# Chunked attention inside a fused transformer block: one exponential per tile, with VectorE subtracting the maximum and summing, in place of eight per-head exponentials

## The chip, the cores and the metric

One Trainium2 chip; the program runs on one core. The metric is device time in microseconds (us) of one execution. The engines are TensorE (PE for its matmuls, PEld for its weight loads), VectorE (DVE), ScalarE (ACT), GpSimd (POOL) and SyncE (SP), which issues the loads and stores.

## The reference

Shortened here. Attention runs within chunks of 64 tokens, for 8 heads of 64 columns, on 8 batches of 576 tokens. Two feed-forward parts follow, a plain one and one gated by a causal convolution.

```python
scores = scale * np.matmul(q_c, k_c.transpose(0, 1, 2, 4, 3))
scores = scores - np.max(scores, axis=-1, keepdims=True)
attn = np.exp(scores)
attn = attn / (np.sum(attn, axis=-1, keepdims=True) + 1e-09)
out = np.matmul(attn, v_c)
...
xn = (x - mu) / np.sqrt(var + 1e-06) * g_ln
ch = np.maximum(xn @ w_ch1, 0.0) @ w_ch2      # x is (8, 576, 512), w_ch1 (512, 2048)
x = x + ch
...
gate = 1.0 / (1.0 + np.exp(-gate_pre))        # gate_pre: causal convolution of x, 5 taps
out = gate * (x @ w_val) @ w_out
```

## The kernel before

The 4608 tokens are cut into 36 tiles of 128 rows (two chunks each); a tile's attention and normalization is called a unit, `unit(u)`. Four units feed one block of 512 tokens, and there are 9 blocks, 0 to 8. Blocks 0 and 1 go through the feed-forward part as plain products (`ffn`), blocks 2 to 8 as seven products of halved matrices (`operands`, `hidden`). After each block comes the convolution and the preparation of the gated part (`conv`, `seven`), and after the last block the gated part itself (`val`, `proj`). Matmul operands are split into a high and a low part, so that each product is three matmuls.

The order of all work is made ahead, by a planner (`Plan`). Every operation is added with an engine, an estimated duration, the operations that it waits for, and a priority; `run` replays this as a greedy schedule, and the instructions are written in the order that comes out. On the chip each engine works through its list in that order and waits on semaphores, so the estimates set the order, and the chip's own durations set the time. The units of a block are planned well ahead of the block, between the products of the blocks before, with priorities that put them ahead of the convolution.

Units 0 to 7 (`u < MERGED`) use an older path. There `smax` (L579) takes the maximum and subtracts it in two DVE instructions, `sexp` (L591) makes one exponential, and the sum of P comes out of a matmul with a column of ones. Units 8 to 35, 28 in all, use the path that the change touches:

- `burst` (L542): one stretch of PE work that writes P times V of the unit before (`pv_plain`) and the scores of this unit into the two banks of one PSUM tile, `att` (64x64 matmuls, L531).
- `peak` (L556, DVE): the maximum of each head's 64 scores (L558), times -1/8 (L559).
- `weigh` (L561, ACT): for each of 8 heads an exponential of 128x64 out of PSUM (L567), with the maximum as bias and the sum of P as accumulator output; the profile shows each as an ACTIVATE and an ACTIVATION_READ_ACCUMULATOR.
- `ev_x` (L606, DVE), for the unit before: reciprocal of the sums, x = (P times V) times it (L616), then the statistics of the normalization (L624 to L627).
- `rstd` (L629, POOL) and `norm` (L633, DVE): xn.
- `tr_p` (L594, PE) turns P by four 128x128 transposes (L504) into the PSUM tile, `ev_p` (L597, ACT) copies it out over P (L598).
- `tr_n` (L639, PE) turns x and xn of the unit before into the same PSUM tile (L504); ACT copies them out (L654, L682).

The tile library adds the waits. It puts PSUM reads of ACT and DVE in the order in which the instructions were written, when they read the same PSUM tile: where x (L616) is written ahead of the first exponential, the exponential waits for it.

Of the kernel before, what the change touches and what calls it, by code (L numbers as in the profile page):

```python
# [9 lines left out]
F32 = mybir.dt.float32  # L10
# [3 lines left out]
AF = mybir.ActivationFunctionType  # L14
ALU = mybir.AluOpType
AX = mybir.AxisListType

P = 128
CH = 64
# [12 lines left out]
class Plan:  # L32
# [8 lines left out]
    def add(self, eng, dur, fn, deps=(), pri=0.0):  # L41
        op = Op(eng if isinstance(eng, tuple) else (eng,), dur, fn, deps, pri, len(self.ops))
        self.ops.append(op)
        return op

    def take(self, tag):

        return self.held.get(tag, [])

    def hold(self, tag, *ops):  # L50
        self.held[tag] = list(ops)
# [55 lines left out]
def chunk_attention_ffn_gated_conv(  # L107
# [21 lines left out]
    nc = tc.nc  # L129
    B, H, S, D = q.shape  # L130
# [9 lines left out]
    HP = H // 2  # L140
    SCALE = 1.0 / float(D) ** 0.5
# [36 lines left out]
    def view(t, shape, dt):  # L178
        n = 1
        for x in shape[1:]:  # L180
            n *= x
        t = t[: shape[0], :n]
        t = t if dt == F32 else t.bitcast(dt)
        names = "abcd"[: len(shape) - 1]
        return t.rearrange(f"p ({' '.join(names)}) -> p {' '.join(names)}", **dict(zip(names, shape[1:])))

    def slot(tag, shape, dt, name):
        if tag in qk_parts:
            return view(qk_room[:, qk_parts[tag] :], shape, dt)
        return pool.tile(shape, dt, tag=tag, name=name)  # L190
# [27 lines left out]
    add, take, hold = plan.add, plan.take, plan.hold  # L218
# [204 lines left out]
    def unit(u):  # L423


        st = {}
        b, o = divmod(u, TB)
        if b == 0:
            pri, qk_pri, v_pri = FIRST + 10 * o, FIRST + 4 * o, FIRST + 4 * o + 6
        elif b == 1:  # L430
            pri = qk_pri = v_pri = when[1, 0] - LEAD_TILE_1 + STEP_TILE_1 * o
        else:
            pri = qk_pri = v_pri = when[b, 0] - LEAD_TILE + STEP_TILE * o if o else when[b - 1, 0] - LEAD_TILE + 4 * STEP_TILE
# [3 lines left out]
        def tag(what):  # L437
            return early.get(u, {}).get(what, what)
# [100 lines left out]
        def by_head(n, at=0):  # L539
            return st["ps"][:, :, at : at + HP * n].rearrange("p par (h d) -> p par h d", d=n)  # L540
# [12 lines left out]
                st["flat"].rearrange("p (h x) -> p h x", x=P), lambda h, hp, c: st["v"][h, c, hp], D, HP * CH  # L553
            )

        def peak():  # L556
            st["mx"] = mx = slot(f"mx{u % 4}", [P, 2, HP, 1], F32, f"mx{u}")
            nc.vector.tensor_reduce(out=mx[:, :, :, 0], in_=by_head(CH), axis=AX.X, op=ALU.max)  # L558
            nc.vector.tensor_scalar_mul(mx, mx, -SCALE)  # L559

        def weigh():  # L561
            st["P"] = p = slot("P", [P, H, CH], F32, f"p{u}")
            st["flat"] = p.rearrange("p h k -> p (h k)")
            st["rs"] = rs = slot(f"rs{u % 4}", [P, 2, HP, 1], F32, f"rs{u}")
            for hp in range(HP):
                for par in range(2):
                    nc.scalar.activation(  # L567
                        out=p[:, 2 * hp + par],
                        in_=st["ps"][:, par, hp * CH : (hp + 1) * CH],
                        func=AF.Exp,  # L570
                        bias=st["mx"][:, par, hp],
                        scale=SCALE,
                        accum_out=st["rs"][:, par, hp],
                    )

        def scores():
            products(st["T", 0], lambda h, hp, c: st["T", 1][h, hp, c * CH : (c + 1) * CH], CH)
# [110 lines left out]
        def op(eng, dur, fn, *deps, p=pri):  # L688
            return add(eng, dur, fn, [d for x in deps for d in (x if isinstance(x, list) else [x])], p)
# [24 lines left out]
        if u < MERGED:  # L714
# [9 lines left out]
            sm = op("DVE", 1450, smax, sc, take(tag("P")), take(f"mx{u % 4}"))  # L724
            ex = op("ACT", 640, sexp, sm)
            tp = op("PE", 450 * cold, tr_p, ex)
# [21 lines left out]
            ready = [eq, ek]  # L748
        bu = op("PE", 1300 if back and ready else 750, burst, ready, back["ready"] if back else [], take(AB))
        if ready:  # L750
            pk = op("DVE", 750, peak, bu, take(f"mx{u % 4}"))
            ex = op("ACT", 2600, weigh, pk, take("P"), take(f"rs{u % 4}"))
            hold(f"mx{u % 4}", ex)

        def turned_probabilities(ox):
            tp = op("PE", 450, tr_p, ex, ox)
            return tp, op("ACT", 600, ev_p, tp)

        ep = None
        if back:  # L760
            got = {}

            def before(ox):
                if not ready:
                    return None, []
                got["tp"], got["ep"] = turned_probabilities([ox])
                return got["tp"], [got["ep"], ex]

            hold("A", bu)
            hold("B", bu)  # L770
            tn = back["rest"](bu, bu, take("A"), before, pri)[1]
            hold("A", tn)
            hold("B", tn)
            ep = got.get("ep")
        elif ready:
            ep = turned_probabilities([])[1]
            hold("A", bu)
            hold("B", bu)
            hold(AB, ep)
# [941 lines left out]
    for u in range(TB):  # L1721
        unit(u)
# [3 lines left out]
    for b, f in fstep:  # L1726
        if b and f == 0:
            for u in range(TB * b + (b > SB), TB * (b + 1) + (b >= SB)):
                unit(u)
            if b >= SB:  # L1730
                operands(b)
        if f == 0:
            halo(b)
        if b < SB:
            ffn(b, f)
            if b == SB - 1 and f % 4 == 3:
                weight_sums(f // 4)
        elif f % 4 == 0:
            hidden(b, f // 4)
        if (b, f) == (0, KF // 2 + 1):  # L1740
            cw_op = conv_taps(when[0, 3 * KF // 4])
        if (b, f) == (NBLK - 1, KF - 4):
            val_weights()
            out_weights()
        if f == KF - 1:
            conv(b)
        if (b, f) == (3, 0):
            seven_again()
# [45 lines left out]
```

## Time and profile before

| | us |
|---|---|
| median of 3 runs (1109.92 to 1115.55) | 1112.54 |
| the profiled execution: time, and span of its instructions | 1117.29, 1115.5 |
| busy in the span: PE, PEld | 1071.5, 943.5 |
| busy in the span: DVE, ACT, POOL | 851.7, 549.6, 26.5 |

The busy time of PE counts matmuls that overlap each other, so how long PE is held up is read from the starts of its instructions and from the waits. The time of the profiled execution lies 0.4% above the median; all times within the trace are us from the start of its span. A wait is put down to the instruction that released it last.

### The profile page before, as it was taken

What the parts mean: (1) busy time and instruction counts of PE and PEld (TensorE: products, weight loads), DVE (VectorE), ACT (ScalarE), POOL (GpSimd) and SP (SyncE); (2) the same over time, 40 slices, a digit from 0 to 9 for tenths busy, and PEclk for the clock granted to TensorE, in tenths of its full rate; (3) what the DMA queues carried; (4) which work ended last, traced back from release to release, by engine and by line L of the source; (5) the groups of instructions that cost most, each with busy time, mean ns of one, the idle gap of its engine ahead of it and who ended that gap; (6) DMA issues with size and microseconds to landing.
All of it is one profiled execution on the core that took longest, in us unless ns stands there. A gap on an engine that the chain in (4) does not pass through costs nothing.

```text
span 1115.5 us, 22827 instructions
## 1 busy us (share of the span) xinstructions
PE 1071.5 (96%) x8801; PEld 943.5 (85%) x8801; DVE 851.7 (76%) x1537; ACT 549.6 (49%) x1313; POOL 26.5 (2%) x50
## 2 busy tenths in 40 slices
PE   5689999999999999999999999999999999999998
PEld 3478877778988888988888898889889898999998
DVE  5789968897966776796677568577756989898775
ACT  5786533345444345545435443453544554665553
POOL 0000000000000000000000000000000000000000
PEclk9889999999999999999999999999999999999999
DMA  9994243766987888999789878788965986999952
GB/s 212 330 307 115 57 115 118 241 203 183 327 249 219 248 300 292 295 286 270 225 241 309 242 215 291 219 243 249 323 188 194 366 327 257 308 338 361 359 173 89
DMA packets 178036, 275.74 MB, mean 247 GB/s; under 512 B 72196, under 2 KB 123400, under 8 KB 177928
## 3 DMA queue, kind: packets, MB, share of 16 engines
q1 hardware_dynamic: 177928, 274.29, 76.4%
q8 instruction: 69, 1.13, 0.4%
q14 instruction: 39, 0.32, 0.1%
HBM read 206.59 MB, written 67.63 MB: 246 GB/s over the span
## 4 chain that ended last, share of the span: by engine, by line
PE 69%; DVE 13%; ACT 8%; DMA 7%; SPq 2%; issue 2%; POOL 0%; ACTq 0%; DVEq 0%; POOLq 0%
PE m L1001 17%; PE v L1001 7%; PE o L1001 6%; ACT p L567 5%; PE att L504 4%; PE yA L1157 3%; PE yB L1157 3%; PE yA L1159 3%; PE yB L1159 3%; PE yA L1158 3%; PE yB L1158 3%; PE h L839 2%; PE h L840 2%; DMA x7d<-x 2%; PE y L862 2%; PE h L841 2%
## 5 line engine op out<-in xcount | busy, mean ns | idle before, releaser
L1001 PEld LDWEIGHTS m<-late,a 128*128 128x128 f32 x2352 | 295.8, 189 | 16.4 <-DVE c_hl L1099 1.5
L1001 PE MATMUL m<-late,a 128*128 128x256 f32 x2352 | 304.3, 281 | 1.9 <-ACT c_hh L1092 1.0
L1346 DVE SCALAR_TENSOR_TENSOR acc<-X,cw_sb,acc 128x516 f32<-128x516 f32 (+1 forms) x144 | 108.0, 753 | 5.2 <-ACT acc L1339 2.2
L567 ACT ACTIVATE p<-att,mx 128x64 f32<-128x64 f32 x224 | 66.6, 324 | 57.6 <-DVE x L616 52.9
L1157 PE MATMUL yB<-h,w 128*128 128x512 f32 x224 | 90.8, 405 | 0.0
L1157 PE MATMUL yA<-h,w 128*128 128x512 f32 x224 | 90.0, 402 | 0.0
L1159 PE MATMUL yB<-h,w 128*128 128x512 f32 x224 | 88.3, 394 | 0.0
L1159 PE MATMUL yA<-h,w 128*128 128x512 f32 x224 | 88.1, 393 | 0.0
L1158 PE MATMUL yA<-h,w 128*128 128x512 f32 x224 | 87.7, 392 | 0.0
L1158 PE MATMUL yB<-h,w 128*128 128x512 f32 x224 | 87.6, 391 | 0.0
L1099 DVE TENSOR_TENSOR c_hh<-c_hh,m 128x512 f32<-128x512 f32 x56 | 38.4, 685 | 46.7 <-PE m L1001 25.4
L1127 ACT ACTIVATE h<-c_hh 128x512 fp32r<-128x512 f32 x56 | 35.4, 632 | 58.5 <-DVE c_hh L1099 58.4
L1092 ACT ACTIVATE c_hh<-m 128x512 f32<-128x512 f32 x56 | 33.5, 597 | 55.8 <-PE m L1001 55.5
L839 PE MATMUL h<-xnt,w 128*128 128x512 f32 x128 | 53.6, 419 | 1.2 <-ACT xnt L671 1.2
L840 PE MATMUL h<-xnt,w 128*128 128x512 f32 x128 | 51.8, 405 | 0.7 <-DVE xnt L675 0.7
L1001 PE MATMUL o<-w,gv 128*128 128x256 f32 x432 | 52.0, 277 | 0.0
L862 PE MATMUL y<-hh,w 128*128 128x512 f32 x128 | 51.6, 403 | 0.0
L841 PE MATMUL h<-xnt,w 128*128 128x512 f32 x128 | 51.5, 402 | 0.0
L1001 PEld LDWEIGHTS o<-w,gv 128*128 128x128 f32 x432 | 50.5, 188 | 0.0
L1159 PEld LDWEIGHTS yA<-h,w 128*128 128x128 f32 x224 | 42.1, 188 | 9.9 <-DVE h L1130 0.4
L1159 PEld LDWEIGHTS yB<-h,w 128*128 128x128 f32 x224 | 42.1, 188 | 9.7
L864 PE MATMUL y<-hl,w 128*128 128x512 f32 x128 | 50.3, 393 | 0.0
(194 smaller groups left out, 2194.7 us busy)
## 6 DMA issues: line engine op xcount, KB each, us to landing
a<-a SPq DMA_DIRECT2D x196, 512.0 KB, 5.1
x7d<-x SPq DMA_DIRECT2D x63, 512.0 KB, 6.0
raw<-in_moe_w_ch_dram SPq DMA_DIRECT2D x32, 512.0 KB, 7.9
late<-x7d SPq DMA_DIRECT2D x24, 512.0 KB, 5.4
qk_room<-in_q_dram SPq DMA_DIRECT2D x100, 112.0 KB, 3.9
qk_room<-in_k_dram SPq DMA_DIRECT2D x100, 112.0 KB, 3.3
v<-in_v_dram SPq DMA_DIRECT2D x144, 64.0 KB, 3.3
out_dram<-os SPq DMA_DIRECT2D x18, 512.0 KB, 5.1
```

Source lines behind the costliest of these rows:

```text
L504: nc.tensor.transpose(ps[:, c], src[:, c], ident)
L567: nc.scalar.activation(out=p[:, 2 * hp + par], in_=st["ps"][:, par, hp * CH : (hp + 1) * CH], func=AF.Exp, bias=st["mx"][:, par, hp], scal ...
L839: nc.tensor.matmul(ps, wh, xh, start=(kk == 0), stop=False)
L840: nc.tensor.matmul(ps, wh, xl, start=False, stop=False)
L841: nc.tensor.matmul(ps, wl, xh, start=False, stop=(kk == KD - 1))
L862: nc.tensor.matmul(ps, wh[:, s], st["hh"], start=opens, stop=False)
L864: nc.tensor.matmul(ps, wh[:, s], st["hl"], start=False, stop=closes)
L1001: nc.tensor.matmul(ps[:, f], l, right(r, k), start=new and f == k == i == 0, stop=k == 1 and i == 2, skip_group_check=True,)
L1157: nc.tensor.matmul(ps, wh, hh, start=opens and f == 0, stop=False)
L1158: nc.tensor.matmul(ps, wl, hh, start=False, stop=False)
L1159: nc.tensor.matmul(ps, wh, hl, start=False, stop=closes and f == 3)
L1346: nc.vector.scalar_tensor_tensor(out=a, in0=X[b][:, f, i : i + L], scalar=cw_sb[:, i, f : f + 1], in1=a, op0=ALU.mult, op1=ALU.add,)
```

## The change

`peak` and `weigh` are no longer used. Units 8 to 35 take the older path's `smax` and `sexp`: DVE takes the maximum and subtracts it, which moves the scores from PSUM to the SBUF tile `P`, and one ACT instruction makes the exponential of all 8 heads in place in SBUF, without an accumulator output. A new DVE instruction (`add_up`) sums each head's 64 values of P into the tile `rs`, which `ev_x` of the next burst reads. Its planned priority is 2000 behind that of the unit. `ev_p` overwrites P, and so gets a wait for the sum.

```diff
-        def peak():
-            st["mx"] = mx = slot(f"mx{u % 4}", [P, 2, HP, 1], F32, f"mx{u}")
-            nc.vector.tensor_reduce(out=mx[:, :, :, 0], in_=by_head(CH), axis=AX.X, op=ALU.max)
-            nc.vector.tensor_scalar_mul(mx, mx, -SCALE)
-
-        def weigh():
-            st["P"] = p = slot("P", [P, H, CH], F32, f"p{u}")
-            st["flat"] = p.rearrange("p h k -> p (h k)")
+        def add_up():
             st["rs"] = rs = slot(f"rs{u % 4}", [P, 2, HP, 1], F32, f"rs{u}")
-            for hp in range(HP):
-                for par in range(2):
-                    nc.scalar.activation(
-                        out=p[:, 2 * hp + par],
-                        in_=st["ps"][:, par, hp * CH : (hp + 1) * CH],
-                        func=AF.Exp,
-                        bias=st["mx"][:, par, hp],
-                        scale=SCALE,
-                        accum_out=st["rs"][:, par, hp],
-                    )
+            nc.vector.tensor_reduce(
+                out=rs[:, :, :, 0], in_=st["P"].rearrange("p (h par) k -> p par h k", par=2), axis=AX.X, op=ALU.add
+            )
...
-            pk = op("DVE", 750, peak, bu, take(f"mx{u % 4}"))
-            ex = op("ACT", 2600, weigh, pk, take("P"), take(f"rs{u % 4}"))
-            hold(f"mx{u % 4}", ex)
+            sm = op("DVE", 1450, smax, bu, take("P"), take(f"mx{u % 4}"))
+            ex = op("ACT", 640, sexp, sm)
+            su = op("DVE", 720, add_up, ex, take(f"rs{u % 4}"), p=pri + 2000.0)
+            hold(f"mx{u % 4}", sm)
...
-            return tp, op("ACT", 600, ev_p, tp)
+            return tp, op("ACT", 600, ev_p, tp, su)
```

The planner makes a new order from this. All engines keep their old order up to unit 8 and again behind unit 35. Three places at unit 22 show the difference. In the names, `mx22`, `p22`, `rs22` and `att22` belong to unit 22, whose burst also finishes unit 21 (`x21`, `xn21`); `c4_2_...`, `h4_2_...`, `m..._4_2` and `yA_4`, `yB_4` are feed-forward work of block 4. In the changed file the lines behind the edit are 13 or 14 smaller (L616 is L602, L598 is L584, L635 is L621, L1099 is L1086).

DVE from the maximum of unit 22 on, before:

```order
L558 TENSOR_REDUCE mx22_5942<-att22_5902 128x8
L559 TENSOR_SCALAR mx22_5942<-mx22_5942 128x8
L613 TENSOR_SCALAR rs21_5798<-rs21_5798 128x8
L614 RECIPROCAL rs21_5798<-rs21_5798 128x8
L616 TENSOR_TENSOR x21_5960<-att22_5902,rs21_5798 128x2x4x64
L624 BN_STATS stat21_5962<-x21_5960 128x6
L626 BN_AGGR mv21_5963<-stat21_5962 128x2
L627 TENSOR_SCALAR ve21_5965<-mv21_5963 128x1
L635 TENSOR_SCALAR xn21_5996<-x21_5960,mv21_5963,rstd21_5989 128x512
L1099 TENSOR_TENSOR c4_2_hh1_5900<-c4_2_hh1_5900,m5_4_2_5945 128x512
```

and in the changed kernel:

```order
L569 TENSOR_REDUCE mx22_5877<-att22_5838 128x8
L570 TENSOR_TENSOR p22_5876<-att22_5838,mx22_5877 128x2x4x64
L599 TENSOR_SCALAR rs21_5745<-rs21_5745 128x8
L600 RECIPROCAL rs21_5745<-rs21_5745 128x8
L602 TENSOR_TENSOR x21_5902<-att22_5838,rs21_5745 128x2x4x64
L610 BN_STATS stat21_5904<-x21_5902 128x6
L612 BN_AGGR mv21_5905<-stat21_5904 128x2
L613 TENSOR_SCALAR ve21_5907<-mv21_5905 128x1
L1086 TENSOR_TENSOR c4_2_hh1_5832<-c4_2_hh1_5832,m5_4_2_5818 128x512
L558 TENSOR_REDUCE rs22_5924<-p22_5876 128x8
L621 TENSOR_SCALAR xn21_5943<-x21_5902,mv21_5905,rstd21_5922 128x512
```

The scaling of the maximum (L559) is replaced by the subtraction (L570), ahead of x. The sum (L558 of the changed kernel) and an addition of the feed-forward (L1086) stand between the statistics and the normalization xn; before, that addition stood behind xn.

ACT around the exponentials of unit 22, before (x8 stands for eight instructions) and in the changed kernel:

```order
L1092 ACTIVATE c4_2_hh1_5900<-m1_4_2_5831 128x512
L567 ACTIVATE p22_5968,rs22_5969<-att22_5902,mx22_5942 128x64 x8
L1092 ACTIVATE c4_2_hl0_5994<-m5_4_2_5945 128x512
L598 ACTIVATE p22_5968<-att22_5902 128x512
L1127 ACTIVATE h4_2_0_5862<-c4_2_hh1_5900 128x2x256
```

```order
L1079 ACTIVATE c4_2_hh1_5832<-m1_4_2_5761 128x512
L1079 ACTIVATE c4_2_hl0_5871<-m5_4_2_5818 128x512
L578 ACTIVATE p22_5876<-p22_5876 128x512
L1114 ACTIVATE h4_2_0_5809<-c4_2_hh1_5832 128x2x256
L584 ACTIVATE p22_5876<-att22_5838 128x512
```

The one exponential (L578) stands behind the two copies of products (L1079), and a copy that waits for the addition L1086 on DVE (L1114) stands between it and the eviction of P (L584).

PE around the transposes of unit 22, before and in the changed kernel:

```order
L1158 MATMUL yB_4_5526<-h4_1_1_5726,w15_1005 128x512
L1159 MATMUL yB_4_5526<-h4_1_1_5727,w15_1005 128x512
L504 MATMUL att22_5902<-ident_66,p22_5968 128x128 x4
L1001 MATMUL m5_4_2_5945<-late1_2958,a4_2_3_5844 128x256 x12
L504 MATMUL att22_5902<-ident_66,x21_5960 128x128 x4
L504 MATMUL att22_5902<-ident_66,xn21_5996 128x128 x4
```

```order
L1145 MATMUL yB_4_5469<-h4_1_1_5650,w15_1005 128x512
L1146 MATMUL yB_4_5469<-h4_1_1_5651,w15_1005 128x512
L504 MATMUL att22_5838<-ident_66,p22_5876 128x128 x4
L988 MATMUL m1_4_2_5761<-late1_2934,a4_2_7_5784 128x256 x12
L504 MATMUL att22_5838<-ident_66,x21_5902 128x128 x4
L504 MATMUL att22_5838<-ident_66,xn21_5943 128x128 x4
```

In both, one product of 12 matmuls stands between the transposes of P and those of x and xn, and 12 matmuls of 512 columns and 12 of 256 between the burst and the transposes of P.

## Rows read from the trace of the kernel before

**Rows 1.** The page's head and its part 1: busy time (share of the span) of each engine.
```profile
span 1115.5 us, 22827 instructions
...
PE 1071.5 (96%) x8801; PEld 943.5 (85%) x8801; DVE 851.7 (76%) x1537; ACT 549.6 (49%) x1313; POOL 26.5 (2%) x50
```

**Rows 2.** Windows: length, busy us (instructions) of PE, PEld, DVE, ACT, POOL, clock, DMA.
```profile
165.00:835.00 670.00, 658.29 (x5603) 576.12 (x5602) 495.01 (x902) 304.31 (x871) 18.80 (x28) 1.00 0.80 249
835.00:1115.50 280.50, 272.20 (x2102) 260.08 (x2100) 224.84 (x375) 145.66 (x262) 0.00 (x0) 1.00 0.77 276
```

**Rows 3.** Waits from 165 to 835 us: engine, waiting line, releaser: total us, times, longest.
```profile
ACT p L567 <- DVE x L616: 52.9, 20, 5.3
...
DVE c_hh L1099 <- PE m L1001: 25.2, 17, 2.5
...
DVE mx L558 <- PE att L531: 20.3, 13, 3.7
...
PEld att L504 <- ACT p L567: 13.9, 17, 1.6
...
PE att L504 <- ACT p L567: 7.1, 17, 1.2
...
PEld att L504 <- ACT p L598: 2.7, 3, 1.5
```

**Rows 4.** Timeline, unit 22, all engines: start us, length us, engine, line, operation [idle before].
```profile
510.61 0.65 PE L531 MATMUL att<-kT,qT 64*64 64x64 f32 x32
...
511.32 0.69 DVE L558 TENSOR_REDUCE mx<-att 128x8 f32<-128x512 f32 x1 [1.26 <-PE att L531]
...
512.05 0.17 DVE L559 TENSOR_SCALAR mx<-mx 128x8 f32<-128x8 f32 x1
...
512.57 0.69 DVE L616 TENSOR_TENSOR x<-att,rs 128x512 f32<-128x512 f32 x1
...
513.37 0.31 ACT L567 ACTIVATE p<-att,mx 128x64 f32<-128x64 f32 x1 [3.27 <-DVE x L616]
...
514.24 0.15 DVE L627 TENSOR_SCALAR ve<-mv 128x1 f32<-128x1 f32 x1
...
514.75 0.40 PE L1157 MATMUL yB<-h,w 128*128 128x512 f32 x1
...
515.20 0.40 PE L1159 MATMUL yB<-h,w 128*128 128x512 f32 x1
...
515.61 0.24 ACT L567 ACTIVATION_READ_ACCUMULATOR p<-att,mx 128x1 f32 x1
...
515.89 0.42 PEld L504 LDWEIGHTS att<-ident,p 128*128 128x128 f32 x4 [0.73 <-ACT p L567]
515.90 0.66 PE L504 MATMUL att<-ident,p 128*128 128x128 f32 x4 [0.30 <-ACT p L567]
...
516.65 0.60 ACT L598 ACTIVATE p<-att 128x512 f32<-128x512 f32 x1 [0.32 <-PE att L504]
...
517.90 0.60 PE L504 MATMUL att<-ident,x 128*128 128x128 f32 x4
```

**Rows 5.** Groups by form: line, engine, operation, count, busy us, mean ns, idle before.
```profile
L567 ACT ACTIVATE p<-att,mx 128x64 f32<-128x64 f32 x224 | 66.6, 324 | 57.6 <-DVE x L616 52.9 <-DVE mx L559 4.7
...
L567 ACT ACTIVATION_READ_ACCUMULATOR p<-att,mx 128x1 f32 x224 | 48.5, 217 | 0.0
...
L475 DVE STREAM_TRANSPOSE qT<-qk_room 128x512 f32<-128x512 f32 x28 | 30.9, 1105 | 9.9 <-PE att L504 5.4 <-DMA qk_room<-in_k_dram 2.4 <-DMA qk_room<-in_q_dram 2.1
...
L558 DVE TENSOR_REDUCE mx<-att 128x8 f32<-128x512 f32 x28 | 19.3, 688 | 20.3 <-PE att L531 20.3
...
L584 DVE TENSOR_TENSOR p<-att,mx 128x512 f32<-128x512 f32 x8 | 5.5, 692 | 0.3
...
L592 ACT ACTIVATE p<-p 128x512 f32<-128x512 f32 x8 | 5.0, 630 | 2.4 <-DVE p L584 2.4
...
L559 DVE TENSOR_SCALAR mx<-mx 128x8 f32<-128x8 f32 x28 | 4.8, 172 | 1.0
```

## The prediction

> **What bounds the kernel now.** I read the page's first part, the windows, the waits of the stretch in which the changed code runs, one tile's timeline, and the groups by form. TensorE (PE) is busy 1071.5 of 1115.5 us, VectorE (DVE) 851.7, ScalarE (ACT) 549.6 [rows 1]. So the kernel ends when PE has worked through its list, and a change on DVE or ACT counts only by what PE waits. All 28 units of the changed path lie between 165 and 835 us. There PE is busy 658.3 of 670 us, which leaves it 11.7 us, while DVE has 175 us idle (670 less 495.0) and ACT 366 [rows 2]. The granted clock is 1.00 from 165 us on [rows 2], the upper of its two levels (2.4 GHz), so nothing is to be had from the clock.
>
> The waits of that stretch name what PE lacks: its transposes of P (L504) wait for the exponentials (L567) in 17 of 28 units, 7.1 us by the matmul row and 13.9 us by the weight-load row [rows 3]. It is the largest wait of PE there. ACT in turn waits 52.9 us before those exponentials, 20 times, for DVE's product x (L616) of the unit before [rows 3].
>
> The timeline of unit 22 shows one such case; most units look like it [rows 4]. The scores begin on PE at 510.61, the maximum on DVE at 511.32, its scaling at 512.05. By 512.22 ACT has the numbers it needs, yet its first exponential starts at 513.37, 0.11 us after x ended (512.57 + 0.69). The last accumulator read ends at 515.85 (515.61 + 0.24), and PE's load for the transposes starts 0.04 us later, at 515.89. PE's matmuls before them started at 514.75 and, two further, at 515.20, one every 0.23 us, so the first transpose could have started at 515.43; it started at 515.90: 0.47 us lost. The weight-load row of the same wait says 0.73 us, so 0.26 us of what that row counts is not lost.
>
> **What the wait is worth.** By the weight-load row, less that part: 13.9 - 17 x 0.26 = 9.5 us. The ends are the two rows themselves, 7.1 and 13.9 us [rows 3]. I take 9.5, because it comes from starts of matmuls, and the two rows differ by how a pipelined matmul's end is drawn.
>
> Here a rule of the Trainium skill speaks (Perfetto Trace Analysis, Identifying the Most-Contended Engine): matmul busy time misjudges how much room TensorE has, since matmuls are pipelined, and the share of weight loads is the better measure. With 7.1 the sum below would be -5.6 us, with the 13.9 that the rule prefers -12.4 us. The spacing of starts lies between them.
>
> **The change part by part** (28 units each).
>
> *ACT.* Eight exponentials with eight accumulator reads leave, 224 of each in all [rows 5]: from 513.37 to 515.85, 2.48 us a unit [rows 4]. One exponential of 128x512 comes, which the first eight units already do in 0.63 us [rows 5]. ACT loses 28 x 1.85 = 52 us of work. It has 366 us idle there; by itself this is worth nothing.
>
> *DVE.* The scaling of the maximum leaves (0.17 us). The subtraction comes: 0.69 us, by the same instruction of the first eight units [rows 5]. The sum of P comes: a reduction of 512 values to 8, from SBUF; no row shows it. The nearest is the maximum, the same reduction from PSUM, 0.69 us; the far end is the 32x32 transpose of 128x512, 1.1 us [rows 5]. I take 0.69 us. DVE gains 28 x 1.21 = 34 us of work against 175 us idle [rows 2]; with the far end it would be 45 us.
>
> *The chain from the scores to the transposes of P*, by unit 22's times. Maximum 511.32 to 512.01, subtraction 512.05 to 512.74, and the rest of DVE's list 0.64 us later than now: x ends at 513.90 instead of 513.26. The exponential reads what the subtraction wrote in SBUF, no longer the PSUM tile that x reads; it starts some 0.11 us after the subtraction and ends at 513.5. The transposes need both, and with the 0.04 us above they are free to go at 513.94. PE comes to them at 515.43: the order still leaves 12 matmuls of 512 columns and 12 of 256 between burst and transposes in unit 22. So the wait goes, with 1.5 us to spare: **-9.5 us**.
>
> *The new wait.* The eviction of P (L598 before) overwrites what the sum reads, so it now waits for the sum. In unit 22 DVE's list behind x is: statistics, to 515.03 (514.24 + 0.15 + 0.64); one addition of the feed-forward, 0.69; the sum, to about 516.50; then the normalization (0.55), to 517.09. The eviction could run from 516.6 to 517.2. PE reaches the transposes of x, which need it, 2.00 us after those of P (515.90 to 517.90 now), at 517.43. The margin is 0.2 us here; where no addition stands ahead of the sum it is 0.9 us. Behind the eviction on ACT stand the copies of that tile and the next feed-forward copies, behind the sum on DVE the normalization, needed at 517.87. I charge 1.5 us over all units for those whose DVE list comes late: in 13 of 28 DVE waits for the scores now, so it was free; in the other 15 it may not be [rows 3]. Bounds: 0, and 28 x 0.2 = 6 us with a sum of 1.1 us, which uses up the margin and 0.2 us more. **+1.5 us.**
>
> *Moved.* The planner shifts the units by 2 to 4 us within the stretch and puts them back before each feed-forward block; from the end of unit 35 on all engines have the old order. No queue gets a load or store more. PE's other waits there, 2.7 us for the eviction of P among them [rows 3], I leave as they are.
>
> **Sum:** -9.5 + 1.5 = -8.0 us. The profiled execution took 1117.29 us (span 1115.5 and 1.8 around it), 4.75 us above the median of the runs, 1112.54. Against its own time: 1109.3; on the median's scale **1104.5 us**, 0.7% faster. About 0.5%, 5.6 us, is what a measurement of this kernel can tell from no change.
>
> **Rivals.**
> 1. *The wait goes, and more than 2.4 us comes back at the additions of the feed-forward.* For: DVE gets 34 us more, and PE's products wait for additions that stand in the same list; against: DVE now idles 25.2 us waiting for PE at just those additions [rows 3]. If half of the 9.5 comes back: 1108 us, no measurable change.
> 2. *Slower: DVE's list per unit becomes what PE waits for.* The place is the sum ahead of the eviction and the normalization. With 1.1 us for the subtraction as well as the sum, the chain is 0.82 us longer than in the sum above, less the margin of 0.2 us gives 0.6 us per unit, 17 us in all: 1112.54 - 9.5 + 17 = 1120 us. It decides from 0.54 us a unit on (9.5 / 28 + 0.2). Against: the subtraction has a row at 0.69, so it takes a slow sum and a late DVE together. The Trainium skill warns of this step (VectorE: DVE Perf Modes, Rules for kernel authors): it calls `tensor_reduce` the slowest VectorE operation, to be restructured when on the hot path, and this change puts a second one per unit there. The trace agrees only that it is no faster than other fp32 passes: 0.69 us for the maximum.
> 3. *The change does more than it says:* all of the 13.9 us and the 2.7 us at the eviction go, and ACT's shorter list helps the copies: 1112.54 - 16.6 = 1096 us.
> 4. *The exponential still waits for x* (the wait has another cause than the shared PSUM tile). Then it would run from 514.0 to 514.64, still 0.5 us before PE needs it: the forecast stands, so this has no chance of its own.
>
> **How the numbers follow.** Forecast, gain of 5.6 to 14 us: 0.62. Rival 1: 0.24. Rival 2: 0.08, of which 0.06 over the bound. Rival 3: 0.06. Faster 0.62 + 0.06 = 0.68; slower 0.06; the rest, 0.26, within 0.5%. The range reaches from 1097.5 (a gain of 15) to 1112, where rival 1 has given back all; rival 2 and the far part of rival 3 are left out.
>
> **What would show it.** Right: no row of PE waiting for the exponential (L578 of the changed kernel), which starts right behind the subtraction and before x ends; PE idle some 6 us instead of 11.7 in the stretch of these units (11.7 - 7.1 + 1.5); DVE some 34 us more there, ACT some 52 less; after 835 the same picture, 8 us earlier. Wrong: PE waiting for the eviction of P or for the normalization in many units, a sum far over 0.69 us, or new waits of PE's products for additions of the feed-forward.

## The result and the profile after

| | before | after |
|---|---|---|
| median of 5 runs each, us | 1114.23 (1109.92 to 1115.55) | 1104.39 (1101.38 to 1106.30) |
| the profiled execution: time and span, us | 1117.29, 1115.5 | 1106.30, 1104.5 |

The ratio is 0.9916, 95% interval 0.9888 to 0.9943: faster by 9.8 us. 1104.5 us was forecast, and faster by over 0.5% was its likeliest outcome. One execution of an experiment further down (e_cost) took 1513 us at a granted clock of 0.655 and is left out of its ratio.

The head and part 1 of the page of the changed kernel answer to [rows 1]:

```profile
span 1104.5 us, 22430 instructions
...
PE 1068.5 (97%) x8801; PEld 946.1 (86%) x8801; DVE 878.5 (80%) x1565; ACT 500.6 (45%) x893; POOL 24.6 (2%) x50
```

The windows of the changed kernel, columns as in [rows 2]; the end of the units' stretch is put 10 us earlier:

```profile
165.00:825.00 660.00, 653.91 (x5591) 577.59 (x5592) 520.91 (x927) 253.49 (x449) 16.90 (x28) 1.00 0.79 252
825.00:1104.50 279.50, 272.81 (x2113) 261.10 (x2112) 226.25 (x378) 147.62 (x264) 0.00 (x0) 1.00 0.77 278
```

PE has 6.1 us idle there, where it had 11.7. Its waits in the changed kernel from 165 to 825 us, beside those of DVE and ACT that [rows 3] showed before:

```profile
ACT p L578 <- DVE rs L599: 33.6, 13, 4.1
DVE mx L569 <- PE att L531: 25.0, 15, 3.1
ACT p L584 <- DVE rs L558: 17.3, 9, 2.8
...
ACT p L578 <- DVE p L570: 15.0, 8, 3.6
...
DVE c_hh L1086 <- PE m L988: 9.5, 12, 2.0
...
PEld att L504 <- ACT p L584: 3.1, 4, 0.9
PE m L988 <- DMA a<-a: 2.5, 2, 2.2
...
PE att L504 <- ACT p L584: 1.6, 4, 0.7
```

No row of PE waiting for the exponential (L578) is left. What PE still waits for at its transposes is the eviction of P (L584), 3.1 us by the load row; the eviction in turn waits 17.3 us for the sum (L558). Unit 22 again, the timeline of the changed kernel, in the columns of [rows 4]:

```profile
512.30 0.65 PE L531 MATMUL att<-kT,qT 64*64 64x64 f32 x32
...
513.74 0.69 DVE L570 TENSOR_TENSOR p<-att,mx 128x512 f32<-128x512 f32 x1
514.35 0.16 DVE L599 TENSOR_SCALAR rs<-rs 128x8 f32<-128x8 f32 x1
...
514.55 0.63 ACT L578 ACTIVATE p<-p 128x512 f32<-128x512 f32 x1 [2.06 <-DVE rs L599]
514.78 0.69 DVE L602 TENSOR_TENSOR x<-att,rs 128x512 f32<-128x512 f32 x1
...
516.90 0.59 PEld L504 LDWEIGHTS att<-ident,p 128*128 128x128 f32 x4
517.13 0.60 PE L504 MATMUL att<-ident,p 128*128 128x128 f32 x4
...
517.49 0.68 DVE L558 TENSOR_REDUCE rs<-p 128x8 f32<-128x512 f32 x1
517.60 0.63 ACT L1114 ACTIVATE h<-c_hh 128x512 fp32r<-128x512 f32 x1 [2.42 <-DVE c_hh L1086]
...
518.26 0.60 ACT L584 ACTIVATE p<-att 128x512 f32<-128x512 f32 x1
...
518.91 0.42 PEld L504 LDWEIGHTS att<-ident,x 128*128 128x128 f32 x4
518.94 0.63 PE L504 MATMUL att<-ident,x 128*128 128x128 f32 x4
```

The exponential starts 0.12 us after the subtraction has ended (513.74 + 0.69 = 514.43) and runs beside x. The profile puts its wait down to L599, which ends 0.08 us after the subtraction on the same engine; what the exponential reads is written by the subtraction. It is done at 515.18, 1.72 us before PE loads P. The other end is tight: the eviction ends at 518.86, and PE's load of x follows 0.05 us later.

**Where PE's time went.** The matmuls between the first score of unit 8 and the last transpose of unit 35 are the same in number and form before and after. So the length of this stretch can be split exactly: the median distance from one start to the next for each form, added up over all matmuls (627.2 us), and what each distance has beyond it, put down to the matmul that started late. Worked out in this way from the starts in each profile (us; e_both has 2.8 us of its products outside the stretch). The column "late: P" is the time that PE lost at its transposes of P. The rows below "after" are the experiments, in words further down:

```
kernel        stretch  late: P     x     m  other
before         668.40   12.42  2.09  3.26  23.40
after          659.32   -0.02  2.52  4.48  25.11
e_again        655.45    0.16  1.45  2.32  24.30
e_less         680.56   26.08  1.18  3.01  23.05
e_mid          658.41    3.81  0.65  2.50  24.22
e_cost         659.95    2.09  1.08  5.01  24.54
e_heads        662.25    1.91  1.64  6.00  25.46
e_told         655.91    0.50  1.01  3.90  23.27
e_told_again   660.88    0.94  2.61  6.90  23.21
e_psum         659.19    0.51  1.41  5.71  24.34
e_twice        661.92   -0.02  7.18  3.31  24.23
e_short        657.68    0.35  0.24  4.64  25.23
e_first        656.90   -0.01  1.03  5.95  22.71
e_both         666.84    0.33  0.84 15.99  25.22
```

P and x are the transposes of P and of x, m the feed-forward products (L988). Of the last column some 17 us are the pattern of starts within the bursts, before and after alike; the rest lies mostly at products of the feed-forward. Of the 9.1 us between before and after, P gave 12.4 and the rest took back 3.4. The changed kernel run twice differs by 3.9 us in this stretch, another version by 5.0: a single profile does not carry differences smaller than that, but a column that goes from 12.4 to 3.8 or less in every version that should empty it does.

### The profile page after: what moved, and what is told of

Its sections match the earlier page's. It is cut to its first block, busy times and chain, and to the rows that moved or that the text cites. A ratio compares the mean times of both kernels' runs of the same rounds, so it can differ in the third digit from the quotient of the medians.

```text
span 1104.5 us, 22430 instructions
## 1 busy us (share of the span) xinstructions
PE 1068.5 (97%) x8801; PEld 946.1 (86%) x8801; DVE 878.5 (80%) x1565; ACT 500.6 (45%) x893; POOL 24.6 (2%) x50
## 4 chain that ended last, share of the span: by engine, by line
PE 84%; DVE 6%; DMA 5%; ACT 2%; SPq 2%; issue 1%; DVEq 0%; ACTq 0%
PE m L988 21%; PE v L988 8%; PE o L988 7%; PE yA L1144 4%; PE yB L1144 4%; PE yA L1146 4%; PE yA L1145 4%; PE yB L1146 4%; PE att L504 4%; PE yB L1145 4%; PE att L531 3%; PE h L826 3%; PE h L827 3%; PE h L828 3%; PE y L849 2%; PE y L851 2%
## 5 line engine op out<-in xcount | busy, mean ns | idle before, releaser
L988 PEld LDWEIGHTS m<-late,a 128*128 128x128 f32 x2352 | 296.6, 189 | 18.8 <-DVE h L1117 2.4
L988 PE MATMUL m<-late,a 128*128 128x256 f32 x2352 | 304.0, 280 | 4.2 <-DMA a<-a 2.5
L1114 ACT ACTIVATE h<-c_hh 128x512 fp32r<-128x512 f32 x56 | 35.3, 630 | 70.1 <-DVE c_hh L1086 69.9
L1086 DVE TENSOR_TENSOR c_hh<-c_hh,m 128x512 f32<-128x512 f32 x56 | 38.4, 686 | 33.0 <-ACT c_hh L1079 22.8
L1079 ACT ACTIVATE c_hh<-m 128x512 f32<-128x512 f32 x56 | 33.4, 596 | 56.2 <-PE m L988 55.7
L849 PE MATMUL y<-hh,w 128*128 128x512 f32 x128 | 51.8, 404 | 0.7 <-ACT hh L834 0.7
L988 PE MATMUL o<-w,gv 128*128 128x256 f32 x432 | 52.0, 277 | 0.0
L988 PEld LDWEIGHTS o<-w,gv 128*128 128x128 f32 x432 | 50.5, 188 | 0.0
L850 PE MATMUL y<-hh,w 128*128 128x512 f32 x128 | 50.1, 391 | 0.0
```

The lines of the kernel that those rows point to most:

```text
L849: nc.tensor.matmul(ps, wh[:, s], st["hh"], start=opens, stop=False)
L850: nc.tensor.matmul(ps, wl[:, s], st["hh"], start=False, stop=False)
L988: nc.tensor.matmul(ps[:, f], l, right(r, k), start=new and f == k == i == 0, stop=k == 1 and i == 2, skip_group_check=True,)
```

## The experiments

The theory: the gain is that PE no longer comes to its transposes of P before the exponentials are done, and nothing else. Both halves of the edit (a shorter exponential, one that need not wait for x) and also a planned order with more products ahead of the transposes would give it. The rivals: ACT's smaller load is what counts, or one half of the edit alone; and for the cost, that the sum on DVE is dear. Each kernel ran beside the kernel before on the same chip, in three groups on three chips, so times are compared by their ratio to the kernel before. No run has the changed kernel's order with the old instructions; the first three experiments come nearest to it. The changed kernel, run once more for comparison (e_again), gave 0.9914 (0.9888 to 0.9940):

> The changed kernel once more, so that the others can be set beside it on the same chip. Both theories: 0.992 of the kernel before, 8 to 10 us faster.

**The plan alone, no instruction changed.** Three kernels change one number of the kernel before, the planned duration of the exponentials (2600 ns):

```diff
-            ex = op("ACT", 2600, weigh, pk, take("P"), take(f"rs{u % 4}"))
+            ex = op("ACT", 3700, weigh, pk, take("P"), take(f"rs{u % 4}"))
```

with 3700 (e_cost), 3200 (e_mid) and 1900 (e_less).

> The kernel before with one number changed: the planned duration of the eight exponentials is 3700 ns in place of 2600 ns. No instruction is added, removed or altered; the planner now puts 5.5 to 6.2 us of products between burst and transposes of P in place of 4.1. Theory (what the change gained is that PE no longer comes to the transposes of P before the exponentials are done, and nothing else): the wait of PE's load for them goes from 13.9 us to under 2 us, and the time falls by 7 to 10 us, as with the change, while ACT stays at some 550 us busy and DVE at some 852 us. Rival (the gain comes from 49 us less work on ACT, or from exponentials that end earlier for ACT's other users): under 3 us faster.

> The kernel before with the planned duration of the eight exponentials at 3200 ns: 4.82 us of products behind the burst in most units, 0.69 more than before, which covers the 0.47 us that PE lost there. Theory (cover just enough is worth as much as the change): 0.987 to 0.993 of the kernel before, PE's wait for the exponentials under 2 us. Rival (half a microsecond is too little cover, or the wait for x makes the exponentials late in ways that no planned length covers): 0.994 to 0.998.

> The kernel before with one number changed the other way: the planned duration of the eight exponentials is 1900 ns in place of 2600. The planner now puts 3.44 us of products between burst and transposes of P in most units, in place of 4.13. Theory (PE waits for whatever of the exponentials the planned distance does not cover): 0.69 us more in each of some 20 to 28 units; PE's load waits for the exponentials 25 to 35 us in place of 13.9, and the time is 8 to 18 us longer than before, 1.007 to 1.016. Rival (the distance is not what counts, the planner's shifts give it back elsewhere): within 4 us of the kernel before.

Measured: with 1900, 1.0107 (1.0089 to 1.0125); with 3200, 0.9929 (0.9909 to 0.9948); with 3700, 0.9935 (0.9912 to 0.9959). The waits with 1900 (from 165 to 830 us, as in all experiments where nothing else is said):

```profile
ACT p L567 <- DVE x L616: 57.1, 21, 5.3
PEld att L504 <- ACT p L567: 28.7, 22, 2.6
PE att L504 <- ACT p L567: 19.7, 20, 2.2
```

with 3200:

```profile
ACT p L567 <- DVE x L616: 54.7, 18, 5.3
PEld att L504 <- ACT p L567: 3.6, 5, 2.2
```

and with 3700, where the page's part 1 shows the old load on DVE and ACT:

```profile
PEld att L504 <- ACT p L567: 1.2, 1, 1.2
```

```profile
PE 1065.3 (97%) x8801; PEld 944.4 (86%) x8801; DVE 848.9 (77%) x1537; ACT 549.3 (50%) x1313; POOL 24.8 (2%) x50
```

In most units 0.69 us of products fewer between burst and transposes makes P 13.7 us later in all, 0.69 us more takes 8.6 of the 12.4 us away, and further products take another 1.7 and add nothing to the time that these runs can tell. The exponentials themselves wait for x as before (57.1 and 54.7 us; [rows 3] had 52.9) and are the same instructions. So 7 to 8 us of gain came without any of ACT's 49 us less work, inside the interval of the changed kernel's gain.

**Each half of the edit alone.** In e_psum the subtraction writes back into the PSUM tile and the one exponential reads it there, so it shares the tile with x again (units 8 to 35; the first eight stay as they are):

```diff
-                out=p.rearrange("p (h par) k -> p par h k", par=2),
+                out=by_head(CH),
...
-            nc.scalar.activation(out=st["flat"], in_=st["flat"], func=AF.Exp, scale=SCALE)
+            nc.scalar.activation(
+                out=p.rearrange("p (h par) k -> p par h k", par=2), in_=by_head(CH), func=AF.Exp, scale=SCALE
+            )
```

> The changed kernel, but the subtraction writes in place into the PSUM tile, and the one exponential reads it from there; the order of all instructions is the changed kernel's. The exponential now shares the PSUM tile with x and in most units waits for it again. Theory (either half of the edit is enough by itself: a short exponential that starts behind x ends some 0.5 to 1.3 us before PE needs it): the exponential starts 0.1 us after x, 0.9 us later than in the changed kernel; no wait of PE for it over 1 us in all; the time within 3 us of the changed kernel. Rival (the start mattered, its length alone would not have done): 5 us or more slower than the changed kernel.

Measured: 0.9918 (0.9896 to 0.9939), no different from the changed kernel. Its timeline in unit 22:

```profile
512.34 0.70 DVE L565 TENSOR_TENSOR att<-att,mx 128x512 f32<-128x512 f32 x1
...
513.38 0.69 DVE L616 TENSOR_TENSOR x<-att,rs 128x512 f32<-128x512 f32 x1
...
514.19 0.60 ACT L572 ACTIVATE p<-att 128x512 f32<-128x512 f32 x1 [3.17 <-DVE x L616]
...
515.43 0.59 PEld L504 LDWEIGHTS att<-ident,p 128*128 128x128 f32 x4
```

The exponential starts 0.12 us after x (514.07), 1.15 us behind the subtraction, and still ends 0.64 us before PE's load. The Trainium skill (PSUM — Partial Sum Buffer, PSUM bank collisions raise a hardware error) says that two engines may not touch the same bank and quadrant of PSUM at once, two readers included, and that software has to keep them apart. The traces agree with the order that follows from it: out of PSUM the exponential stands behind x, out of SBUF it runs beside it (514.55 to 515.18 and 514.78 to 515.47 above). What an overlap would do was not tried.

In e_heads the subtraction stays in SBUF, and eight exponentials by head sum as they go, so DVE makes no sum:

```diff
-            ex = op("ACT", 640, sexp, sm)
-            su = op("DVE", 720, add_up, ex, take(f"rs{u % 4}"), p=pri + 2000.0)
+            ex = op("ACT", 640, by_heads, sm, take(f"rs{u % 4}"))
```

> The changed kernel, but after the subtraction by VectorE eight exponentials by head, in place in SBUF, each with the sum as accumulator output, in the same planned place; no sum on DVE, and the eviction of P waits for none. Theory (the exponential's start mattered, since it no longer waits for x; its length of 2.5 us against 0.63 us did not): exponentials from 0.1 us after the subtraction, 2.4 to 2.6 us long, done some 0.1 us before PE needs them; time within 3 us of the changed kernel, 0.990 to 0.995 of the kernel before. Rival (the length of the exponentials mattered): PE waits for them again in most of 28 units, 0.2 to 0.5 us each, so 5 to 10 us slower than the changed kernel.

Measured: 0.9960 (0.9944 to 0.9977), half of the gain. The theory's time missed, and the rival's reason did not hold either, as the waits show (L561 is the exponentials, L1079 a copy of a product):

```profile
PEld m L988 <- ACT c_hl L1079: 4.2, 5, 1.0
...
PEld att L504 <- ACT p L561: 1.8, 6, 0.4
```

The timeline before one of the five waits:

```profile
342.94 1.56 PE L988 MATMUL m<-late,a 128*128 128x256 f32 x12
...
343.82 0.26 ACT L561 ACTIVATE p<-p 128x64 f32<-128x64 f32 x1 [2.75 <-DVE rs L600]
...
345.66 0.19 ACT L561 ACTIVATION_READ_ACCUMULATOR p<-p 128x1 f32 x1
345.75 0.57 ACT L1079 ACTIVATE c_hl<-m 128x512 f32<-128x512 f32 x1
346.38 1.33 PEld L988 LDWEIGHTS m<-late,a 128*128 128x128 f32 x11 [0.93 <-ACT c_hl L1079]
```

The product ended at 344.50; its copy stood behind the exponentials until 345.75, and the next product waited for the copy. The planner had been told 0.64 us for 2.03 us of work (343.82 to 345.85). If that is the cause, the right number must cure it (e_told: 2600 in place of 640, nothing else):

> The kernel with the subtraction by VectorE and eight exponentials by head in SBUF once more (no sum on DVE), with one number changed: the planner is told 2600 ns for them in place of 640 ns (they took 2.02 us in the run before). Theory (what counts is that the planner reckons with at least the time that the chip takes; 2 us of exponentials then cost nothing): the products' waits for copies that stand on ACT behind the exponentials go, and the time comes to 0.990 to 0.994 of the kernel before. Rival (half of the gain needs the short exponential, because ACT's list is too full at these places whatever the order): 0.995 to 0.998 again.

> The kernel with the subtraction on DVE, eight exponentials by head in SBUF and 2600 ns planned for them, once more, beside the others on the same chip. Theory and rival alike: 0.987 to 0.991 of the kernel before; if it comes out at 0.991 or more, it is no better than the changed kernel.

Measured: 0.9889 (0.9866 to 0.9913), and in the second run 0.9930 (0.9908 to 0.9952). The waits for that copy are gone in both profiles (the second has one of 1.9 us for another copy, c_hh). 2 us of exponentials cost nothing that these runs can tell where the plan knows of them: the two runs of this kernel lie on either side of the changed kernel. That the waits for the copy were all that e_heads lost is not shown, since column m, 6.00 there, is 3.90 and 6.90 in the two profiles of the cure.

**The price of the sum.** e_twice makes the sum twice (`add_up_twice` calls `add_up` and writes the same sum once more):

```diff
-            su = op("DVE", 720, add_up, ex, take(f"rs{u % 4}"), p=pri + 2000.0)
+            su = op("DVE", 720, add_up_twice, ex, take(f"rs{u % 4}"), p=pri + 2000.0)
```

e_short sums one value of each head's 64:

```diff
-                out=rs[:, :, :, 0], in_=st["P"].rearrange("p (h par) k -> p par h k", par=2), axis=AX.X, op=ALU.add
+                out=rs[:, :, :, 0], in_=st["P"].rearrange("p (h par) k -> p par h k", par=2)[:, :, :, :1], axis=AX.X, op=ALU.add
```

and e_first plans the sum at the unit's own priority:

```diff
-            su = op("DVE", 720, add_up, ex, take(f"rs{u % 4}"), p=pri + 2000.0)
+            su = op("DVE", 720, add_up, ex, take(f"rs{u % 4}"))
```

> The changed kernel with the sum of P made twice, the second time over the first: 0.68 us more on DVE per unit ahead of the eviction of P and of the normalization, 19 us in all; the order is the changed kernel's. Theory (the sum stands 0.2 to 0.4 us ahead of what PE waits for, in about 11 units, and in some 6 units it is waited for already): PE waits 0.3 us in the eleven and 0.7 us in the six, 4 to 10 us slower than the changed kernel, all of it before the transposes of x, released by the eviction of P. Rival (there is slack enough): within 2 us of the changed kernel.

> The changed kernel with a sum over 1 of each head's 64 values (63 of 64 are left out of it); same order, the instruction takes some 0.1 to 0.2 us in place of 0.68. It prices the sum. Theory (the sum costs the 1.4 to 2.5 us that PE waits before the transposes of x): 1 to 3 us faster than the changed kernel, and the waits for the eviction of P gone. Rival (the sum delays also the normalization and the additions of the feed-forward, and PE's products by them): 4 us or more faster.

> The changed kernel with the sum at the unit's own priority in place of 2000 behind it, so that it is planned ahead of the addition of the feed-forward on DVE. Theory (the delay at the eviction is small, and the additions have room of their own, since DVE waits for PE there): within 2 us of the changed kernel, 0.990 to 0.993 of the kernel before; the waits of PE for the eviction of P fall to under 1 us. Rival (the additions are what PE's products need next): 3 us or more slower, with PE waiting for additions.

Measured: e_twice 0.9957 (0.9942 to 0.9971), e_short 0.9903 (0.9879 to 0.9927), e_first 0.9907 (0.9883 to 0.9931). The waits of e_twice, where the eviction is L593:

```profile
PEld att L504 <- ACT p L593: 7.9, 12, 1.5
PE att L504 <- ACT p L593: 4.4, 10, 1.1
```

The second sum adds 0.68 us to each unit's list on DVE, 19 us in all, and costs 0.4%, some 4.6 us; column x of the table has it (7.18, which is 4.7 to 5.7 more). So the slack ahead of the eviction is real but small. A sum of 0.16 us empties column x (0.24); the sum costs 1.2 to 2.3 us there. Its time, and that of e_first, cannot be told from the changed kernel's.

**Slack where none is needed.** e_both is the changed kernel with 2600 ns planned for the one exponential of 0.63 us, so that the transposes stand as late as in e_told. The line stands twice in the file, and both were changed: units 0 to 7 are planned with 2600 too, and PE's order differs from the changed kernel's from 17 us on:

```diff
-            ex = op("ACT", 640, sexp, sm)
+            ex = op("ACT", 2600, sexp, sm)
...
-            ex = op("ACT", 640, sexp, sm)
+            ex = op("ACT", 2600, sexp, sm)
```

> The changed kernel, with one number changed: the planner is told 2600 ns for the one exponential (0.63 us on the chip), so that the transposes of P stand where they stand with eight exponentials by head and the right length. Theory (short or long exponential makes no difference once the plan covers it; what is left between versions is the sum on DVE and chance of order): 0.987 to 0.993, within 3 us of that version. Rival (the short exponential is worth something by itself, where it has room): 0.986 or less.

Measured: 1.0006 (0.9989 to 1.0022). The whole gain is gone; theory and rival both missed. Its waits from 262 to 284 us:

```profile
PEld m L988 <- ACT late L1020: 5.9, 2, 5.5
PE m L988 <- ACT late L1020: 5.1, 1, 5.1
PEld m L988 <- DVE late L1024: 3.6, 2, 2.9
PE m L988 <- DVE late L1024: 3.1, 2, 2.7
```

The units lose nothing (P 0.33, x 0.84). At one place, the start of block 2, the first products wait for their operands, which ACT (L1020) and DVE (L1024) split too late: 8.2 us by the matmul rows. Column m is 15.99. That the planner, which believed ACT occupied, put those splits elsewhere was read from the plan's rule, and not tested apart. Nor is it shown which units' number moved them: e_told has 2600 in units 8 to 35 alone, and no product waits for these splits in either of its profiles, so the number of units 0 to 7, which the expectation did not reckon with, may be what did it.

## Why the prediction was right

- **The mechanism.** Shown: the wait of [rows 3] for L567 is gone, and moving the transposes in the plan, with every instruction as before, moves the time by +1.1% and -0.7%.
- **Its size, -9.5 us, was too small.** By starts it was 12.4 us: 11.3 us at the first of the four transposes, in 19 units with 0.17 to 1.35 us each, and 1.1 us between the four. The step that failed is "13.9 - 17 x 0.26": the 0.26 us of unit 22 was taken from all 17 waits. The load row, 13.9 us, was nearer than my correction of it; the matmul row, 7.1, was far off. The rule of the Trainium skill that the prediction weighed (Perfetto Trace Analysis, Identifying the Most-Contended Engine) speaks of busy shares; carried over to the two rows of a wait, as the prediction did, it was the better guide.
- **The new wait, +1.5 us.** Its size was right: 1.2 to 2.3 us by e_short. At the same place 2.1 us went that had stood there before, and that the prediction left as they were, so column x hardly moved (2.09 to 2.52, 1.45 in the second profile). In the one profile another 2.9 us came back at feed-forward products, 2.2 of it at one late load; in the second profile of the same kernel nothing did. In the first profile the errors offset each other: -12.4 and +3.4; in the second nothing did, -12.3 and -0.7. That -8.0 forecast came so near to -9.8 measured is in part luck.
- **The chain of unit 22.** The exponential's start, 0.11 us after the subtraction: 0.12. Transposes free with 1.5 us to spare behind x: 1.62 (517.13 less 515.47 and 0.04). The difference is a slip of the prediction: it lets x end 0.64 us later, where its own lines give 0.69 - 0.17 = 0.52, as measured (from 2.65 to 3.17 us behind the first score). The eviction's margin of 0.2 us was used up, though unit 22 lost nothing by it: PE's load follows 0.05 us behind the eviction, the shortest distance of all units, as in the four where PE waits. The eviction ended where it was forecast, 6.56 us behind the first score for 6.59; what was mis-sized is PE's way from the transposes of P to those of x, 1.81 us (517.13 to 518.94) for 2.00. The copy L1114 (517.60 to 518.23) stands ahead of the eviction on ACT, but the sum sets its start: it starts 0.09 us after the sum, as in unit 8, where ACT had been free for 2 us. With the second sum of e_twice PE waits there in 12 units.
- **The loads.** ACT lost 49.0 us of the 52 said. The sum took 0.68 us for 0.69. DVE gained 26.8 us by part 1 of the page for 34 said: neighbouring instructions overlap in it by some 0.08 us (L599 starts at 514.35, the subtraction ends at 514.43), which the product of counts and durations leaves out; with overlaps counted twice the gain is 32.6 us.
- **PE idle** 6.1 us for 6 said. Behind unit 35, where the order is the same in all kernels, PE needs 278.7 us before, 276.2 after and 277.7 in the second profile; over all profiles it is 275.9 to 281.3, so this says nothing of the change.
- **The rivals.** The first (half comes back at the additions) is not seen: additions (L1086) wait less for PE, 9.5 us for 25.2, and PE hardly for them. The second put the turning point at 0.54 us more per unit; 0.68 us more cost only 4.6 us (0.16 us a unit), because PE waits for the eviction only 12 times in 28 units. The third (all of the 13.9 us and the 2.7 us at the eviction go) was near in its first part, 12.4 us; the second part went and was replaced by the sum's, and 1096 us was not reached. The fourth was tried (e_psum): the exponential waits for x, and the time stays, as said.

## What to carry to other kernels

Where an order is planned ahead, a wait of the bound engine can mean that one duration in the plan is too short: raise that number first, by as much as the trace shows to be late, before any instruction is made faster. Here 2600 ns covered the exponentials' own 2.48 us, but the plan knew of no wait for x, by which they started 1.15 us late in unit 22 (512.22 to 513.37 in [rows 4]). Raising such a number can cost as much elsewhere as it gives, as e_both showed, so the new profile is to be read as a whole. And work that is moved to an idle engine costs what it delays on that engine's list ahead of the bound one, here 1 to 2 us of 19.

## What the runs showed that was not expected

Eight exponentials of the same size are shorter in e_heads, where they read SBUF and take no maximum as bias. The groups by form of e_heads, where [rows 5] had 324 and 217 ns out of PSUM and with the bias:

```profile
L561 ACT ACTIVATE p<-p 128x64 f32<-128x64 f32 x224 | 54.0, 243 | 45.2 <-DVE rs L600 35.2 <-DVE p L571 8.2 <-DVE rs L601 1.7
L561 ACT ACTIVATION_READ_ACCUMULATOR p<-p 128x1 f32 x224 | 42.0, 187 | 0.0
```

For eight that is 2.03 us in place of 2.48. The single exponential of 128x512 goes the other way: 596 ns out of PSUM in e_psum, 631 in place in SBUF in the changed kernel. What makes them differ was not tried.

The sum (677 ns, out of SBUF) is no slower than the subtraction of the same 128x512 (692 ns, out of PSUM, as the maximum with its 688 in [rows 5]), as these groups of the changed kernel show:

```profile
L570 DVE TENSOR_TENSOR p<-att,mx 128x512 f32<-128x512 f32 x36 | 24.9, 692 | 1.4
...
L558 DVE TENSOR_REDUCE rs<-p 128x8 f32<-128x512 f32 x28 | 19.0, 677 | 0.0
```

So the sentence of the Trainium skill behind the second rival (VectorE: DVE Perf Modes, Rules for kernel authors: `tensor_reduce` is the slowest operation) is not borne out at this shape in fp32; the transpose of 128x512 in [rows 5] takes 1105 ns.
